# Leaky values kept in PSUM in the first block, and the last quadrant's ScalarE passes moved into the next slot

## The chip, the cores and the metric

The kernel runs on one NeuronCore of a Trainium2 chip. Its engines are TensorE (PE in the profile, its weight loads PEld), VectorE (DVE), ScalarE (ACT), GpSimd (POOL) and SyncE (SP, which issues most DMAs here). Each engine works through its own instructions in the order in which the program issues them, and waits on semaphores for the others. The metric is the device time of one execution in microseconds; before the change it is 1990.66 us, the median of three runs (1990.62 to 1990.68).

## The reference

A gated scan over time feeds a two-layer MLP with a leaky activation. In short:

```python
sig = 1.0 / (1.0 + np.exp(-f_logit))          # (4, 6080, 256)
f = lower_bound + (1.0 - lower_bound) * sig
h = f[:, t] * h + (1.0 - f[:, t]) * x[:, t]   # for t in range(6080); y[:, t] = h
x = y.reshape(24320, 256)
h = x @ w_in                                  # (256, 2048)
out = np.maximum(0.01 * h, h) @ w_out         # (2048, 256)
```

All of it is float32. The kernel reaches that precision on TensorE by splitting each operand into a high part (rounded to fp32r by a write of that type) and a low part (the value less its high part), and by summing three products: low weight by high value, high by high, high by low.

## The kernel before, in words

**Tiling.** The 24320 tokens are cut into 24 blocks of 1024 (the last has 768); a block's two halves of 512 are the columns of the matmuls. The 2048 hidden features are cut into 8 groups of 256. A *slot* is one group of one block; its hidden values are four *quadrants* of 128 features by 512 tokens, written (h, t) with h the feature half and t the token half. There are 192 slots, in order of block and group (the list `seq`, line 364).

**A quadrant's way.** Its sum h ends in a PSUM bank or an SBUF tile. Two ScalarE passes follow: `leaky_high` (L352) writes the leaky value rounded to fp32r, gh, to SBUF; `leaky` (L357) writes the leaky value in full float32. VectorE's `low` (L362) subtracts the two and gives gl. Six matmuls (`second`, L290) then take gh and gl to the output banks o. Three of a slot's four second products run in the next slot (`old`), one (0, 0) at the end of its own.

**Blocks 1 to 23 (`slot`, L428)** use a scheme of Strassen's kind: seven products M1 to M7 of three matmuls each (L268) instead of eight, over three banks a, b and c. PE's order in a slot is M1 (a), M5 (c), M2 (b), M6 (a), six matmuls of old (1, 1), M7 (a), six of old (1, 0), M4 (a), six of old (0, 1), M3 (c), six of second (0, 0). Bank a accumulates through M1, M6, M7 and M4; between them ScalarE copies the state to SBUF (c11 after M1, L438; c12 after M6, L445; c22 after M7, L450), so that M6 waits for c11's copy, M7 for c12's, M4 for c22's. VectorE adds the banks b and c to these (L442, L451, L469). The last quadrant (0, 1) is complete at L469, after M3; its passes stand at lines 473 and 474 and its low part at 476, at the end of the slot.

**The first block (`plain_slot`, L400, and `first_slots`, L530)** has no prepared sums of weights yet and takes eight plain products in each slot. In it the weights arrive: they are loaded raw, ScalarE prepares them in two passes (`scale_w`, L104 and L106), VectorE masks and joins them (`decode_w`, L112 and L113), POOL adds the two parts (L118), ScalarE rounds the high part (`split_w`, L127) and VectorE takes the low part (L129). For group g this is done for w_in of the next group and for w_out of its own. Also the weight sums for the later blocks are formed (`combine_w`, L134 to L138, and `split_c`, L144 and L145), one group in each slot from slot 6 of block 0 to slot 6 of block 1.

**Preparing the next block.** Transposes, gate, scan, differences and splits of block j + 1 are spread over the slots of block j by a table of hooks, keyed by slot and place. The places "C", "a0", "A", "W", "B", "a3", "D", "V" and "E" are calls in the slot's code. "a0" holds one ScalarE pass of 1024 columns in each of slots 2 and 3 (Tanh, L214) and 6 and 7 (rounding, L235). Block 0 uses the copy `late` of the table, with two places changed.

**The order** is written out by hand: inside `tc.manual_schedule()` every engine runs its instructions in the order of the code. Semaphores follow from which tile or bank is read and written. Tiles come from pools: a new tile of a tag takes the buffer that was given back first, and waits for its last reader. The tag "c" has four SBUF buffers, and in the program before c11 always lies where the previous slot's c11 lay, c12 where its c22 lay, c22 where its c21 lay. Bank a is a pair of PSUM buffers, b and c are one each; the output banks are four more.

Of the kernel before, what the change touches and what calls it, by code (L numbers as in the profile page):

```python
# [8 lines left out]
F32 = mybir.dt.float32  # L9
# [15 lines left out]
def tile_gated_scan_then_leaky_mlp(  # L25
# [13 lines left out]
    P = 128  # L39
# [54 lines left out]

    def scale_w(kind, g, hs=slice(0, 2)):
        if (kind, g) not in part_t:
            a = dw_p.tile([P, 2, 256], F32, tag="a", name="a", bufs=2)
            r = dw_p.tile([P, 2, 256], U32, tag="r", name="r")
            w = dw_p.tile([P, 4, P], F32, tag="w", name="w", bufs=2)
            part_t[kind, g] = a, r, w  # L100
        a, r, _ = part_t[kind, g]

        hi, lo = raw_t[kind, g][:, hs, :, 1], raw_t[kind, g][:, hs, :, 0]
        act(out=a[:, hs], in_=hi.bitcast(F32), func=ACTF.Abs, scale=2.0 ** -112)  # L104

        act(out=r[:, hs], in_=lo, func=ACTF.Copy, scale=2.0 ** -29)  # L106
# [22 lines left out]
            vtt(out=wl, in0=w, in1=wh.bitcast(F32), op=ALU.subtract)  # L129

    def combine_w(g):
        w = dw_p.tile([P, 4, P], F32, tag="a", name="a", bufs=2)
        c = dw_p.tile([P, 4, P], F32, tag="w", name="c", bufs=2)
        vtt(out=w, in0=wi_h[:, g, 0:4].bitcast(F32), in1=wi_l[:, g, 0:4].bitcast(F32), op=ALU.add)  # L134
        vtt(out=c[:, 0], in0=w[:, 2], in1=w[:, 3], op=ALU.add)
        vtt(out=c[:, 2], in0=w[:, 0], in1=w[:, 2], op=ALU.subtract)
        vtt(out=c[:, 1], in0=c[:, 0], in1=w[:, 0], op=ALU.subtract)
        vtt(out=c[:, 3], in0=w[:, 1], in1=c[:, 1], op=ALU.subtract)  # L138
        part_t["c", g] = c
# [114 lines left out]
    }  # L254
    late = dict(hooks)
    late[1, "E"] = late.pop((1, "A"))
    late[2, "A"], late[2, "E"] = hooks[2, "A"][:1], hooks[2, "A"][1:]

    hooks_own = {(0, "C"): [("l", (5, 7))]}

# [102 lines left out]

    seq = [(j, g) for j in range(NB) for g in range(NG)]

    def new_c():
        return c_p.tile([P, HM], F32, tag="c", name="c")

# [13 lines left out]
                    plain_halves(bank, j, g, h, t, k, order, rnd)  # L382

    def plain_leaky(j, g, h, t, bank):
        c = new_c()
        leaky_high((j, g, h, t), bank)
        leaky((j, g, h, t), c, bank)
        return c

    def plain_bank(h, t):  # L390
        pool, tag = (ps_b, "bc"[h == 0]) if t else (ps_a, "a")
# [8 lines left out]
    def plain_slot(s, hook):  # L400
        j, g = seq[s]
        hook("C")
        p11 = plain_quad(j, g, 0, 0)
        if s == 2:
            second(j, 1, 0, 0)
        c11 = plain_leaky(j, g, 0, 0, p11)
        hook("a0")
        hook("A")
        hook("W")
        old(s, 1, 1)  # L410
        low((j, g, 0, 0), c11)
        c22 = plain_leaky(j, g, 1, 1, plain_quad(j, g, 1, 1))
        hook("B")
        old(s, 1, 0)
        low((j, g, 1, 1), c22)
        c21 = plain_leaky(j, g, 1, 0, plain_quad(j, g, 1, 0))
        hook("a3")
        hook("D")
        old(s, 0, 1)
        low((j, g, 1, 0), c21)  # L420
        b = plain_quad(j, g, 0, 1)
        hook("V")
        c12 = plain_leaky(j, g, 0, 1, b)
        second(j, g, 0, 0)
        low((j, g, 0, 1), c12)
        hook("E")

    def slot(s, hook):  # L428
        j, g = seq[s]
        n = sizes[j] // 2  # L430
        done = g == 0 and j > 0
        a = ps_a.tile([P, HM], F32, tag="a", name="pa")
        b = ps_b.tile([P, HM], F32, tag="b", name="pb")
        c = ps_b.tile([P, HM], F32, tag="c", name="pc")
        product(a, j, g, M1, True)
        hook("C")
        c11 = new_c()
        act(out=c11[:, :n], in_=a[:, :n], func=ACTF.Copy)  # L438
        product(c, j, g, M5, True)
        product(b, j, g, M2, True)  # L440
        hook("a0")
        vtt(out=c11[:, :n], in0=b[:, :n], in1=c11[:, :n], op=ALU.add)  # L442
        product(a, j, g, M6, False)
        c12 = new_c()
        act(out=c12[:, :n], in_=a[:, :n], func=ACTF.Copy)  # L445
        hook("A")
        old(s, 1, 1)
        product(a, j, g, M7, False)
        c22 = new_c()
        act(out=c22[:, :n], in_=a[:, :n], func=ACTF.Copy)  # L450
        vtt(out=c22[:, :n], in0=c[:, :n], in1=c22[:, :n], op=ALU.add)  # L451
        leaky_high((j, g, 0, 0), c11)
        leaky((j, g, 0, 0), c11, c11)
        old(s, 1, 0)
        if done:
            evacuate(j - 1, 0)
        low((j, g, 0, 0), c11)
        hook("B")
        leaky_high((j, g, 1, 1), c22)
        leaky((j, g, 1, 1), c22, c22)  # L460
        low((j, g, 1, 1), c22)
        product(a, j, g, M4, False)
        c21 = new_c()
        leaky_high((j, g, 1, 0), a)
        leaky((j, g, 1, 0), c21, a)
        old(s, 0, 1)
        hook("a3")
        product(c, j, g, M3, False)
        vtt(out=c12[:, :n], in0=c[:, :n], in1=c12[:, :n], op=ALU.add)  # L469
        low((j, g, 1, 0), c21)  # L470
        if done:
            evacuate(j - 1, 1)
        leaky_high((j, g, 0, 1), c12)
        leaky((j, g, 0, 1), c12, c12)
        second(j, g, 0, 0)
        low((j, g, 0, 1), c12)
        hook("E")


# [50 lines left out]
    def first_slots(hook):  # L530

        j, g = 0, 0
        h0, h1 = slice(0, 1), slice(1, 2)
        keep_busy(5)
        turn_first(0, 0)
        keep_busy(2)
        turn_first(1, 0)
        keep_busy(4)
        scale_w("i", 0, h0)
        decode_w("i", 0, h0)  # L540
        gate_first(0, 0)
        u_first(0, 0)
        split_w("i", 0, "hl", h0)
        scale_w("i", 0, h1)
        scan_first(0, 0)
        decode_w("i", 0, h1)
        gate_first(1, 0)
        u_first(1, 0)
        high(0)
        lower(0)  # L550
        split_w("i", 0, "h", h1)
        p11, p21 = plain_bank(0, 0), plain_bank(1, 0)
        plain_halves(p11, j, g, 0, 0, 0, (1, 0, 2))
        turn_first(0, 1)
        scale_w("i", 1)
        scan_first(1, 0)
        split_w("i", 0, "l", h1)
        plain_halves(p21, j, g, 1, 0, 0, (1, 2, 0))
        turn_first(1, 1)
        high(1)  # L560
        lower(1)
        decode_w("i", 1)
        gate_first(0, 1)
        u_first(0, 1)
        gate_first(1, 1)
        u_first(1, 1)
        plain_halves(p11, j, g, 0, 0, 1)
        plain_halves(p21, j, g, 1, 0, 1)
        scan_first(0, 1)
        split_w("i", 1, "hl")  # L570
        scan_first(1, 1)

        q11, q21 = (ps_b.tile([P, HM], F32, tag=tag, name="p" + tag) for tag in "bc")
        keep_busy(3, q11)
        plain_rounds(((0, q11), (1, q21)), j, 1, 0, ((1, 2), (0,)))
        leaky_high((j, g, 0, 0), p11)
        high(3)
        c11 = new_c()
        leaky((j, g, 0, 0), c11, p11)
        high(2)  # L580
        lower(3)
        lower(2)
        p22, p12 = (ps_o.tile([P, HM], F32, tag=tag, name="p" + tag) for tag in ("o10", "o11"))
        plain_rounds(((1, p22), (0, p12)), j, g, 1, ((0, 1), (2,)))
        scale_w("o", 0)
        c21 = plain_leaky(j, g, 1, 0, p21)
        decode_w("o", 0)
        load_w("i", 2)
        load_w("o", 1)
        load(1, "l")  # L590
        load_w("o", 2)
        load(1, "x")
        low((j, g, 0, 0), c11)
        q22, q12 = (ps_a.tile([P, HM], F32, tag="a", name="pa") for _ in range(2))
        for h, q in ((1, q22), (0, q12)):
            for k in range(KC):
                plain_halves(q, j, 1, h, 1, k)
        c22 = plain_leaky(j, g, 1, 1, p22)
        low((j, g, 1, 0), c21)
        split_w("o", 0, "hl")  # L600
        scale_w("i", 2)
        decode_w("i", 2)
        load_w("i", 3)
        low((j, g, 1, 1), c22)
        c12 = plain_leaky(j, g, 0, 1, p12)
        low((j, g, 0, 1), c12)
        last_state(0, 0)
        last_state(0, 1)
        second(j, 0, 0, 0)
        hook("C")  # L610
        d11 = plain_leaky(j, 1, 0, 0, q11)
        hook("V")
        second(j, 0, 1, 0)
        d21 = plain_leaky(j, 1, 1, 0, q21)
        low((j, 1, 0, 0), d11)
        hook("W")
        second(j, 0, 1, 1)
        d22 = plain_leaky(j, 1, 1, 1, q22)
        low((j, 1, 1, 0), d21)
        second(j, 0, 0, 1)  # L620
        d12 = plain_leaky(j, 1, 0, 1, q12)
        low((j, 1, 1, 1), d22)
        low((j, 1, 0, 1), d12)
        hook("E")

    with tc.manual_schedule():
# [18 lines left out]
        for s in range(1, len(seq)):  # L645
            j, g = seq[s]

            def hook(at):
                if j == 0:

                    if at == "C":
                        scale_w("o", g)
                        decode_w("o", g)
                        if 1 < g < NG - 1:
# [68 lines left out]
```

## Time and profile before

| What | Value |
|---|---|
| Median of three runs | 1990.66 us |
| The profiled execution's own time | 1990.47 us |
| Its span, first to last instruction | 1988.7 us |
| PE busy | 1977.7 us, 99% of the span |
| PEld / DVE / ACT busy | 82% / 72% / 71% |
| POOL busy | 27.0 us, all in the first 100 us |
| Granted TensorE clock | 1.00 |

Times in the lines of the profile are microseconds from the first instruction, then the duration; "out<-in" names the tiles, and a bracket at the end gives the idle time of the engine before the instruction and what ended it. A matmul's duration includes the time in which it drains beside the next one, so the distance between starts tells what it costs: some 0.229 us for 512 columns. A slot of blocks 2 to 22 takes 10.30 us, 45 matmuls. In the list of groups a row gives the line, the engine, the operation, the tiles with shapes, the count, the busy time with the mean in ns, and the idle time before.

### The profile page before, as it was taken

Reading aid. Unit: us, or ns where it says so; the run is one execution under the profiler, and the core shown is the slowest. Engines: PE = TensorE matmul, PEld = TensorE weight load, DVE = VectorE, ACT = ScalarE, POOL = GpSimd, SP = SyncE. Lnnn points to the kernel's source line nnn. Section 1 sums busy time; section 2 is a strip of 40 time slices with the busy share of each in tenths; the row PEclk is TensorE's granted clock in tenths of the full one; section 3 lists DMA queues with packets and bytes.
Section 4 is the critical chain, followed back from the end, with each engine's and each line's share of the span. In section 5 each row is a group of like instructions: output and inputs, shape, how many; then the busy total and the mean of one; then the engine's idle time right before and its main releaser. Section 6 shows DMA issues by size and latency. Waiting matters only on the chain.

```text
span 1988.7 us, 23487 instructions
## 1 busy us (share of the span) xinstructions
PE 1977.7 (99%) x8820; PEld 1631.3 (82%) x8820; DVE 1422.2 (72%) x2001; ACT 1403.3 (71%) x2354; POOL 27.0 (1%) x25
## 2 busy tenths in 40 slices
PE   8999999999999999999999999999999999999999
PEld 7787888888888888888888888888888888888889
DVE  7987777776777767777677776777767767676664
ACT  7777677667776677766777767776677676776665
POOL 2300000000000000000000000000000000000000
PEclk9999999999999999999999999999999999999999
DMA  9650431504415144051450514505135042340110
GB/s 191 106 64 10 55 49 15 64 13 52 53 11 64 16 48 58 7 64 21 44 62 3 64 23 41 64 0 64 29 36 64 1 64 33 32 54 1 22 22 17
DMA packets 579010, 84.63 MB, mean 43 GB/s; under 512 B 567888, under 2 KB 576848, under 8 KB 578896
## 3 DMA queue, kind: packets, MB, share of 16 engines
q1 hardware_dynamic: 577552, 82.34, 32.7%
q8 instruction: 69, 1.13, 0.2%
q10 hardware_dynamic: 1344, 0.79, 0.1%
q14 instruction: 45, 0.37, 0.1%
HBM read 58.20 MB, written 24.90 MB: 42 GB/s over the span
## 4 chain that ended last, share of the span: by engine, by line
PE 97%; DVE 1%; ACT 0%; issue 0%; DMA 0%; POOL 0%; ACTq 0%; DVEq 0%; POOLq 0%
PE o L290 50%; PE pa L268 26%; PE pc L268 13%; PE pb L268 7%; PE o L309 2%; DVE gl L362 0%; DMA xld<-in_x_dram 0%; DVE xT L180 0%; DVE wi_l L129 0%; POOL w L118 0%; PE po L268 0%; DVE xT L211 0%; DVE lT L211 0%; DVE a L113 0%; PE po L507 0%
## 5 line engine op out<-in xcount | busy, mean ns | idle before, releaser
L290 PE MATMUL o<-gh,wo 128*128 128x512 f32 x2944 | 791.1, 391 | 0.0
L362 DVE TENSOR_TENSOR gl<-c,gh 128x512 fp32r<-128x512 f32 (+1 forms) x768 | 527.7, 691 | 280.9 <-ACT c L357 280.9
L290 PEld LDWEIGHTS o<-gh,wo 128*128 128x128 f32 x2944 | 552.8, 188 | 121.4
L352 ACT ACTIVATE gh<-c 128x512 fp32r<-128x512 f32 (+1 forms) x552 | 342.3, 620 | 168.6 <-DVE c L469 162.2
L290 PE MATMUL o<-gl,wo 128*128 128x512 f32 x1472 | 458.6, 393 | 0.0
L357 ACT ACTIVATE c<-c 128x512 f32<-128x512 f32 (+1 forms) x552 | 346.4, 627 | 17.5
L290 PEld LDWEIGHTS o<-gl,wo 128*128 128x128 f32 x1472 | 276.5, 188 | 59.8
L268 PE MATMUL pa<-yl,wi_h 128*128 128x512 f32 (+1 forms) x768 | 300.9, 392 | 0.1
L268 PE MATMUL pa<-yh,wi_l 128*128 128x512 f32 (+1 forms) x768 | 297.4, 387 | 3.0 <-ACT c L357 1.7
L268 PE MATMUL pa<-yh,wi_h 128*128 128x512 f32 (+1 forms) x768 | 299.5, 390 | 0.6 <-ACT yh L235 0.6
L450 ACT ACTIVATE c<-pa 128x512 f32<-128x512 f32 (+1 forms) x184 | 109.3, 594 | 181.4 <-PE pa L268 178.5
L445 ACT ACTIVATE c<-pa 128x512 f32<-128x512 f32 (+1 forms) x184 | 109.4, 594 | 181.2 <-PE pa L268 180.8
L451 DVE TENSOR_TENSOR c<-pc,c 128x512 f32<-128x512 f32 (+1 forms) x184 | 126.0, 685 | 99.0 <-ACT c L450 94.9
L442 DVE TENSOR_TENSOR c<-pb,c 128x512 f32<-128x512 f32 (+1 forms) x184 | 126.0, 685 | 92.0 <-PE pb L268 79.3
L469 DVE TENSOR_TENSOR c<-pc,c 128x512 f32<-128x512 f32 (+1 forms) x184 | 126.2, 686 | 74.0 <-PE pc L268 73.5
L268 PEld LDWEIGHTS pa<-yh,wi_l 128*128 128x128 f32 x768 | 144.2, 188 | 36.9 <-ACT c L357 2.1
L268 PEld LDWEIGHTS pa<-yh,wi_h 128*128 128x128 f32 x768 | 144.2, 188 | 32.7 <-ACT yh L235 0.7
L268 PEld LDWEIGHTS pa<-yl,wi_h 128*128 128x128 f32 x768 | 144.4, 188 | 28.0 <-DVE yl L238 0.5
L268 PE MATMUL pc<-yl,wi_h 128*128 128x512 f32 (+1 forms) x382 | 149.6, 392 | 0.0
L268 PE MATMUL pc<-yh,wi_h 128*128 128x512 f32 (+1 forms) x382 | 148.9, 390 | 0.0
L268 PE MATMUL pc<-yh,wi_l 128*128 128x512 f32 (+1 forms) x382 | 147.7, 387 | 0.0
L352 ACT ACTIVATE gh<-pa 128x512 fp32r<-128x512 f32 (+1 forms) x200 | 115.8, 579 | 5.2 <-PE pa L268 4.6
(96 smaller groups left out, 1758.9 us busy)
## 6 DMA issues: line engine op xcount, KB each, us to landing
out_dram<-osb SPq DMA_DIRECT2D x184, 128.0 KB, 3.2
lld<-in_f_logit_dram SPq DMA_DIRECT2D x91, 256.0 KB, 5.9
xld<-in_x_dram SPq DMA_DIRECT2D x91, 256.0 KB, 5.8
rawld<-in_moe_w_out_dram SPq DMA_DIRECT2D x6, 512.0 KB, 4.6
raw<-in_moe_w_in_dram SPq DMA_DIRECT2D x8, 256.0 KB, 4.5
rawld<-in_moe_w_in_dram SPq DMA_DIRECT2D x8, 256.0 KB, 3.0
raw<-in_moe_w_out_dram SPq DMA_DIRECT2D x2, 512.0 KB, 3.7
lld<-in_f_logit_dram SPq DMA_DIRECT2D x4, 192.0 KB, 4.5
```

The source lines that it names most:

```text
L268: nc.tensor.matmul(out=bank[:, :n], lhsT=a[:, g, w, :], rhs=b[:, i, :n], start=start and e == 0, stop=stop and e == len(order) - 1, skip_g ...
L290: nc.tensor.matmul(out=o[k][:, :n], lhsT=wo[:, g, h, w, k * P:(k + 1) * P], rhs=v[:, :n], start=first and s == 0, stop=last and s == 2, sk ...
L309: nc.tensor.matmul(out=o[:, u % 2 * D:(u % 2 + 1) * D], lhsT=v[:, u * P:(u + 1) * P], rhs=wo[:, g, h, w, :],  start=first and e == 0 and u ...
L352: act(out=gh[:, :n], in_=src[:, :n], func=ACTF.Prelu, alpha=0.01)
L357: act(out=dst[:, :n], in_=src[:, :n], func=ACTF.Prelu, alpha=0.01)
L362: vtt(out=gl[:, :n], in0=c[:, :n], in1=gh[:, :n].bitcast(F32), op=ALU.subtract)
L442: vtt(out=c11[:, :n], in0=b[:, :n], in1=c11[:, :n], op=ALU.add)
L445: act(out=c12[:, :n], in_=a[:, :n], func=ACTF.Copy)
L450: act(out=c22[:, :n], in_=a[:, :n], func=ACTF.Copy)
L451: vtt(out=c22[:, :n], in0=c[:, :n], in1=c22[:, :n], op=ALU.add)
L469: vtt(out=c12[:, :n], in0=c[:, :n], in1=c12[:, :n], op=ALU.add)
```

## The change

Four things change.

In the first block, `leaky` writes its full value back into the PSUM bank that it reads, and `low` reads it there; no tile of the tag "c" is used for it. The bank then stays in use until `low` has read it. In `plain_slot` the low part of quadrant (0, 0) is issued right behind its passes, ahead of the hooks "a0", "A" and "W".

The tiles a and r of `scale_w` take buffers of the tag "c" instead of tags of their own (r had one buffer, a two), and the tag "a", now used by `combine_w` alone, has one buffer.

In slot 1 of block 0 the calls of the hooks "C", "V" and "W" are written out: the split of w_in 2 now stands ahead of the decoding of w_out 1 and of the first pair of passes, where it stood behind these passes. In slot 2 of block 0 the two transposes of x move from place "E" to place "A".

In blocks 1 to 23 the passes and the low part of quadrant (0, 1) are put into a list `late_c` and issued in the next slot: the passes right behind c11's copy, the low part right behind L442. The last slot of all keeps the old place.

```diff
     def scale_w(kind, g, hs=slice(0, 2)):
         if (kind, g) not in part_t:
-            a = dw_p.tile([P, 2, 256], F32, tag="a", name="a", bufs=2)
-            r = dw_p.tile([P, 2, 256], U32, tag="r", name="r")
+            a = c_p.tile([P, 2, 256], F32, tag="c", name="a")
+            r = c_p.tile([P, 2, 256], U32, tag="c", name="r")
...
     def combine_w(g):
-        w = dw_p.tile([P, 4, P], F32, tag="a", name="a", bufs=2)
+        w = dw_p.tile([P, 4, P], F32, tag="a", name="a")
...
     late[1, "E"] = late.pop((1, "A"))
-    late[2, "A"], late[2, "E"] = hooks[2, "A"][:1], hooks[2, "A"][1:]
...
     def plain_leaky(j, g, h, t, bank):
-        c = new_c()
         leaky_high((j, g, h, t), bank)
-        leaky((j, g, h, t), c, bank)
-        return c
+        leaky((j, g, h, t), bank, bank)
+        return bank
...
-        c11 = plain_leaky(j, g, 0, 0, p11)
+        low((j, g, 0, 0), plain_leaky(j, g, 0, 0, p11))
         hook("a0")
         hook("A")
         hook("W")
         old(s, 1, 1)
-        low((j, g, 0, 0), c11)
...
         act(out=c11[:, :n], in_=a[:, :n], func=ACTF.Copy)
+        for key, src in late_c:
+            leaky_high(key, src)
+            leaky(key, src, src)
         product(c, j, g, M5, True)
         product(b, j, g, M2, True)
         hook("a0")
         vtt(out=c11[:, :n], in0=b[:, :n], in1=c11[:, :n], op=ALU.add)
+        for key, src in late_c:
+            low(key, src)
+        late_c.clear()
         product(a, j, g, M6, False)
         c12 = new_c()
         act(out=c12[:, :n], in_=a[:, :n], func=ACTF.Copy)
...
-        leaky_high((j, g, 0, 1), c12)
-        leaky((j, g, 0, 1), c12, c12)
-        second(j, g, 0, 0)
-        low((j, g, 0, 1), c12)
+        if s + 1 < len(seq):
+            second(j, g, 0, 0)
+            late_c.append(((j, g, 0, 1), c12))
+        else:
+            leaky_high((j, g, 0, 1), c12)
+            leaky((j, g, 0, 1), c12, c12)
+            second(j, g, 0, 0)
+            low((j, g, 0, 1), c12)
         hook("E")
...
-        c11 = new_c()
-        leaky((j, g, 0, 0), c11, p11)
+        leaky((j, g, 0, 0), p11, p11)
...
-        hook("C")
+        scale_w("o", 1)
+        split_w("i", 2, "hl")
+        decode_w("o", 1)
         d11 = plain_leaky(j, 1, 0, 0, q11)
-        hook("V")
         second(j, 0, 1, 0)
         d21 = plain_leaky(j, 1, 1, 0, q21)
         low((j, 1, 0, 0), d11)
-        hook("W")
+        split_w("o", 1, "hl")
```

More of the change, by code (lines that the diff above doesn't have):

```diff
@@ L364, in tile_gated_scan_then_leaky_mlp @@
     seq = [(j, g) for j in range(NB) for g in range(NG)]
+    late_c = []
     def new_c():
@@ L592, in first_slots @@
         load(1, "x")
-        low((j, g, 0, 0), c11)
+        low((j, g, 0, 0), p11)
         q22, q12 = (ps_a.tile([P, HM], F32, tag="a", name="pa") for _ in range(2))
@@ L649, in hook @@
                 if j == 0:
-                    if at == "C":
+                    if at == "C" and g > 1:
                         scale_w("o", g)
```

## The prediction

> **What bounds the kernel now.** I read the page first (the share of each engine), then who waited for whom on PE, then busy time by stretch, and last the timeline around each wait of PE.
>
> ```profile
> span 1988.7 us, 23487 instructions
> PE 1977.7 (99%) x8820; PEld 1631.3 (82%) x8820; DVE 1422.2 (72%) x2001; ACT 1403.3 (71%) x2354; POOL 27.0 (1%) x25
> ...
> PE pa L268 <- DVE wi_l L129: 1.2, 1, 1.2
> PEld pa L268 <- ACT c L438: 2.1, 5, 0.5
> PEld pc L268 <- DVE c L451: 0.9, 3, 0.4
> ...
> 186.80:1834.80 1648.00, 1648.00 (x7202) 1352.25 (x7201) 1171.08 (x1607) 1164.39 (x1921) 0.00 (x0) 1.00 0.33 39
> ```
>
> PE sets the time. In blocks 2 to 21 (the last row) it is busy all 1648.00 us, so nothing can be won there; what a change can win are the few waits in blocks 0 and 1. A wait costs more than the idle time shown, and this event of block 1 gives the rule:
>
> ```profile
> 124.60 0.58 ACT L438 ACTIVATE c<-pa 128x512 f32<-128x512 f32 x1
> ...
> 124.94 0.40 PE L268 MATMUL pb<-yl,wi_h 128*128 128x512 f32 x1
> ...
> 125.23 0.19 PEld L268 LDWEIGHTS pa<-yh,wi_l 128*128 128x128 f32 x1 [0.33 <-ACT c L438]
> ...
> 125.57 0.39 PE L268 MATMUL pa<-yh,wi_h 128*128 128x512 f32 x1
> ```
>
> ScalarE's copy ends at 125.18 and the weight load that waits for it starts 0.05 later. A matmul follows the one before at 0.229 (0.46 for the two at 1035.01, below); here two took 125.57 - 124.94 = 0.63 where 0.46 is due: 0.17 lost. So a weight load that starts L after the last matmul's start delays PE by L - 0.12 (0.29 - 0.12). By the starts of the matmuls the five waits on L438 cost 1.29 and two on L451 0.38 (the groups' idle, 2.1 and 0.9, less 0.16 for each event), together **1.67 us in block 1**.
>
> **The part in later blocks, which decides.** A full slot of block 2 and later, on ScalarE (ACT) and PE (this is slot 2 of a block):
>
> ```profile
> 1030.90 0.63 ACT L352 ACTIVATE gh<-c 128x512 fp32r<-128x512 f32 x1 [0.91 <-DVE c L469]
> 1031.57 0.63 ACT L357 ACTIVATE c<-c 128x512 f32<-128x512 f32 x1
> 1031.81 0.39 PE L268 MATMUL pa<-yl,wi_h 128*128 128x512 f32 x1
> 1032.24 0.60 ACT L438 ACTIVATE c<-pa 128x512 f32<-128x512 f32 x1
> 1032.73 1.05 ACT L214 ACTIVATE lT<-lT 128x1024 f32<-128x1024 f32 x1
> 1034.30 0.60 ACT L445 ACTIVATE c<-pa 128x512 f32<-128x512 f32 x1 [0.51 <-PE pa L268]
> 1035.01 0.62 PE L290 MATMUL o<-gl,wo 128*128 128x512 f32 x2
> 1035.24 0.19 PEld L268 LDWEIGHTS pa<-yh,wi_l 128*128 128x128 f32 x1
> 1035.47 0.39 PE L268 MATMUL pa<-yh,wi_l 128*128 128x512 f32 x1
> 1037.51 0.63 ACT L357 ACTIVATE c<-c 128x512 f32<-128x512 f32 x1
> 1038.05 0.62 ACT L352 ACTIVATE gh<-c 128x512 fp32r<-128x512 f32 x1
> ...
> 94.07 2.01 ACT L235 ACTIVATE yh<-lT 128x1024 fp32r<-128x1024 f32 x2
> 95.96 0.72 ACT L144 ACTIVATE wi_h<-c 128x128 fp32r<-128x128 f32 x2
> ```
>
> Before, the last quadrant's two passes (1030.90, 1031.57) lie ahead of the copy c11 (L438), in time in which ScalarE has nothing else: the copy starts at 1032.24, 0.04 after M1's last matmul ends (1031.81 + 0.39), so PE sets it. Taking the passes from in front of it wins nothing here.
>
> After, they stand between that copy and the hook "a0", and the hook's 1024-wide pass and then the copy c12 (L445) queue behind them. From start to start: copy to next 0.49 (1032.24 to 1032.73); first pass to second 0.66 (it waits for the end, 1030.90 to 1031.57); second pass to the next 0.54 (1037.51 to 1038.05); a 1024-wide pass 0.94 (1.89 for two, 94.07 to 95.96). So c12's copy starts at 1032.24 + 0.49 + 0.66 + 0.54 + 0.94 = 1034.87 instead of 1034.30, and ends 0.60 later, at 1035.47.
>
> Product M7 writes the bank that this copy reads, and its weight load stands at 1035.24, with the last matmul before it started at 1035.01 + 0.23 = 1035.24. Now the load starts at 1035.47 + 0.05 = 1035.52: L = 0.28, and PE loses 0.28 - 0.12 = **0.16 us**. Without a pass in the hook the copy could start 0.94 sooner, at 1033.93, before M6 ends, and nothing is lost.
>
> The hook "a0" holds such a pass in slots 2, 3 (Tanh, L214) and 6, 7 (L235) of each block that prepares a full next block. Rows of blocks 2 to 21:
>
> ```profile
> L235 ACT ACTIVATE yh<-lT 128x1024 fp32r<-128x1024 f32 x40 | 42.1, 1052 | 0.0
> L214 ACT ACTIVATE lT<-lT 128x1024 f32<-128x1024 f32 x40 | 42.1, 1052 | 0.0
> L235 ACT ACTIVATE yh<-xT 128x1024 fp32r<-128x1024 f32 x20 | 21.0, 1052 | 0.0
> ```
>
> In "a0" are all 40 Tanh, the 20 of yh<-xT and half of the 40 of yh<-lT (the other half is in "A", behind c12's copy): 80 slots, 80 x 0.16 = **+12.8 us**. In block 22 the next block is three quarters as long, its pass at least 0.2 shorter, and the loss is gone.
>
> Nothing makes up for it: PE has no other wait there, and every later step of a slot moves with PE. On VectorE the late low part (L362) goes behind L442 and pushes the hook "A" back by 0.6; in slot 5 L451 then comes some 0.6 later, but M3, which needs it, has about 1 us of room. The quadrant's gh and gl are read only by the next slot's second-last group of matmuls, over 3 us after the late pass.
>
> **Block 1.** Its waits on L438 go, since the copy no longer stands behind passes that wait for a late VectorE; VectorE starts each slot's sums 0.6 or more sooner, which ends the two on L451: -1.67. The same M7 loss comes in slots 2, 3, 6, 7: +0.64. In slots 2 and 3 there is more behind c12's copy:
>
> ```profile
> 126.73 1.23 ACT L217 ACTIVATE lT<-lT,cd,cc 128x1024 f32<-128x1024 f32 x1
> 127.87 0.71 ACT L144 ACTIVATE wi_h<-c 128x128 fp32r<-128x128 f32 x2
> ```
>
> From c12's copy start to c22's copy it is then 0.49 + 1.14 + 0.61 = 2.24, 0.59 past M7's end, and M4 waits for it: +0.18 each. Block 1: -1.67 + 0.64 + 0.36 = **-0.67**.
>
> **Block 0.** The rows:
>
> ```profile
> 15.60 1.28 POOL L118 TENSOR_TENSOR w<-a,r 128x512 uint32<-128x512 uint32 x1 [4.41 <-ACT lT L511]
> 16.34 0.69 DVE L517 SCALAR_TENSOR_TENSOR xT<-lT,po 128x512 f32<-128x512 f32 x1 [0.31 <-ACT lT L512]
> ...
> 26.59 2.39 DVE L362 TENSOR_TENSOR gl<-c,gh 128x512 fp32r<-128x512 f32 x2
> 26.85 1.59 POOL L118 TENSOR_TENSOR w<-a,r 128x512 uint32<-128x512 uint32 x1 [2.62 <-DVE a L113]
> 29.18 3.35 SPq L156 DMA_DIRECT2D xld<-in_x_dram  x2
> 30.32 1.30 POOL L118 TENSOR_TENSOR w<-a,r 128x512 uint32<-128x512 uint32 x1 [1.88 <-DVE a L113]
> 30.98 0.63 PE L290 MATMUL o<-gl,wo 128*128 128x512 f32 x2
> 33.31 0.50 PE L268 MATMUL pa<-yh,wi_l 128*128 128x512 f32 x1 [1.70 <-ACT c L357]
> 45.99 0.19 PEld L268 LDWEIGHTS pa<-yh,wi_l 128*128 128x128 f32 x1 [0.48 <-DVE wi_l L129]
> 102.51 0.69 DVE L362 TENSOR_TENSOR gl<-c,gh 128x512 fp32r<-128x512 f32 x1 [0.56 <-ACT c L357]
> 103.19 0.39 PE L268 MATMUL pc<-yh,wi_l 128*128 128x512 f32 x1
> ...
> xld<-in_x_dram SPq DMA_DIRECT2D x91, 256.0 KB, 5.8
> ```
>
> A low part with both inputs in SBUF that meets POOL's sum takes 1.7 to 1.8 (the pair at 26.59 takes 2.39) and stretches POOL to 1.59; a VectorE instruction with one input in PSUM runs in 0.69 beside POOL's 1.28. With its values in PSUM the low part gets that second price, and POOL 1.30. Against it: the second pass, in place, now waits for the first (0.03 behind its end, not 0.10 ahead: +0.14 each), and a bank is free only after the low part, not after the pass.
>
> By rows the first wait, at 33.31, grows: POOL's sum for w_in 2 ends at 28.15, its split on ScalarE 28.18 to 28.81, on VectorE 28.87 to 29.55; now VectorE's two steps for w_out 1 come behind that, to 30.62, POOL 30.78 to 32.08 (before to 31.62), the split of w_out 1 on ScalarE 32.11, passes of quadrant 22 32.64 and 33.25 to 33.84, and on VectorE, behind the w_out split and one low part, the low part that frees the bank 34.00 to 34.69. Weight load 34.74 instead of 33.31: loss 34.74 - 31.21 - 0.12 = 3.41 instead of 1.98. The waits at 45.99 (0.33) and 58.44 (1.46) go: the w_in splits end at about 46.4 and 57.6, PE wants them at 47.2 and 58.2. Adding 0.03 at the bank of p11: -0.33. At 103.19 product M5 takes the bank of the last quadrant, whose low part ends at 103.20; PE and the passes come 0.35 sooner and 0.13 later, so M5 now waits about +0.29. The earlier r pass (its tile no longer waits for POOL) and the two transposes are in these times. The transposes come some 7 us sooner, at about 39.5, ahead of the w_out 2 split on VectorE, which holds back POOL's w_in 3 to 43.6 to 44.9 (its split is the 46.4 above); no DMA moves with them, and the x load that they need is issued by 32.53 and lands some 5.8 after its issue, by 38.4. Without that room PE would wait there for what is missing. Block 0: **-0.04**. What has no row is the pass from PSUM to PSUM: rows have 0.59 out of PSUM and 0.63 out of SBUF; I take 0.59, bounds 0.55 and 0.63, a few hundredths on each link, with other slips -0.7 to +1.0 for the block.
>
> **Sum:** 12.8 - 0.67 - 0.04 = +12.1. The profiled execution took 1990.47 (1.77 more than its span), the median of the runs shown is 1990.66; so 2002.6 to 2002.8: **2002.7 us**, 0.6% slower.
>
> **Rivals.**
> - *Hidden after all* (not slower). Place: M7's weight load, in 80 slots. If ScalarE's line from c11's to c12's copy is 0.16 shorter than counted (each of its five steps 0.03), the load is in time: 1990.66 - 1.67 - 0.04 = 1988.95. For it: 0.16 is little beside a line of 3.2. Against: its pitches repeat within 0.02 over hundreds of slots. 10%.
> - *A buffer wait*. c12's new tile would take the buffer that the late low part still reads: from L442's start 2.32 after M1's, low part 2.93 to 3.61, copy 3.64 to 4.24 where 3.96 is in time: 0.28 in 175 full slots, +49 in place of 13.4: 2038. Against: in the program before, the new c12 takes the buffer of the previous slot's c22, which is long free. 4%.
> - *A slow clock* after the long pause at 31 to 34.7: should PE run at half pitch for as long as it paused, some 13 matmuls cost 0.23 more each, +3.0: 2005.7. Against: the 1.70 pause before left the next matmuls at 0.39, with the granted clock 1.00. 5%. The Trainium skill, "TensorE: Matmul & The Clock Gate", section "Why this matters for your kernels", asks for no pause over about 3 us, or the clock falls to half; the trace before has no pause that long.
> - *All waits gone, nothing added*: 3.77 in block 0 and 1.67 in block 1 off: 1985.2, the floor. 2%.
>
> **How the numbers follow.** The forecast has 79%. Its own range: 0.12 to 0.20 in 80 slots is 9.6 to 16.0, with blocks 0 and 1 within -0.7 to +1.5: 1998.8 to 2007.4. 0.2% is 4 us, about what can be told from no change. Slower by more: the forecast, the buffer wait, the slow clock, 88%; within: the hidden case, 10%; faster by more: 2%. The range 1998 to 2008 leaves out the hidden case, the buffer wait and the floor, 16%.
>
> **What would show it.** Right: in slots 2, 3, 6, 7 of each block a wait of pa's weight load on ACT L445, 80 or more times, and the other slots at 10.30; no waits on L438; one longer wait at 31 us, now on VectorE's L362; L362 near 0.69 in block 0. Wrong: no wait on L445, or one in all slots (then the buffer).

## The result, and the profile after

The changed kernel takes **2003.67 us** (median of 6, 2002.03 to 2005.97) against 1990.68 for the kernel before beside it (median of 6): a ratio of 1.0066, 95% interval 1.0055 to 1.0076. It is 0.66% slower; predicted were 2002.7 and slower. The profiled execution took 2003.66, its span is 2001.9. Among the runs below, one execution took far longer than its nine fellows (2025.11, with the late passes in half the slots); no trace shows why, and the ratio given there leaves it out.

In the profile after, the helpers' lines are one lower than before: L267 is the products, L289 the second products, L351 and L356 the two passes, L361 the low part. In a slot c11's copy is L438 as before, c12's is L451 (was L445), c22's L456 (was L450). First come two lines of the page, and then the waits of PE's weight loads that the change made or altered (idle time of the load in us, number, longest):

```profile
span 2001.9 us, 23578 instructions
PE 1990.7 (99%) x8820; PEld 1626.0 (81%) x8820; DVE 1384.4 (69%) x2001; ACT 1375.5 (69%) x2354; POOL 22.2 (1%) x25
```

```profile
PEld pa L267 <- ACT c L451: 25.0, 84, 0.3
PEld pa L267 <- DVE gl L361: 3.6, 2, 3.4
...
PEld pa L267 <- ACT c L456: 0.6, 2, 0.3
PEld pc L267 <- DVE gl L361: 0.3, 1, 0.3
```

The five waits on c11's copy and the three on VectorE's sum (two of which had cost PE time) are gone, and 84 waits on c12's copy are new: 80 in blocks 2 to 21 and 4 in block 1. PE still counts as busy for 99%, because the wait of a weight load hides in the drain of the matmul before it; its busy time grew from 1977.7 to 1990.7 with the same 8820 matmuls.

How much they cost, by the first copy c11 of blocks 1, 2 and 22, in the timeline of before and then of after:

```profile
103.44 0.60 ACT L438 ACTIVATE c<-pa 128x512 f32<-128x512 f32 x1 [0.96 <-ACT c L357]
...
187.64 0.60 ACT L438 ACTIVATE c<-pa 128x512 f32<-128x512 f32 x1
...
1835.64 0.60 ACT L438 ACTIVATE c<-pa 128x512 f32<-128x512 f32 x1
```

```profile
104.61 0.60 ACT L438 ACTIVATE c<-pa 128x512 f32<-128x512 f32 x1 [0.92 <-PE pa L267]
...
188.14 0.60 ACT L438 ACTIVATE c<-pa 128x512 f32<-128x512 f32 x1 [2.24 <-PE pa L267]
...
1848.80 0.60 ACT L438 ACTIVATE c<-pa 128x512 f32<-128x512 f32 x1 [2.24 <-PE pa L267]
```

From block 2 to 22 it was 1648.00 and is 1660.66: **+12.66, or 0.158 for each of the 80 slots**. Block 1 is 0.67 shorter (83.53 for 84.20). Up to block 1 the kernel has lost 1.17. The rest, blocks 22 and 23, is the same: the end is 13.2 later.

One of the 80 slots, on ScalarE and at product M7:

```profile
1039.07 0.60 ACT L438 ACTIVATE c<-pa 128x512 f32<-128x512 f32 x1 [2.24 <-PE pa L267]
1039.57 0.62 ACT L351 ACTIVATE gh<-c 128x512 fp32r<-128x512 f32 x1
1040.22 0.63 ACT L356 ACTIVATE c<-c 128x512 f32<-128x512 f32 x1
1040.76 1.05 ACT L214 ACTIVATE lT<-lT 128x1024 f32<-128x1024 f32 x1
1041.71 0.57 ACT L451 ACTIVATE c<-pa 128x512 f32<-128x512 f32 x1
1041.85 0.62 PE L289 MATMUL o<-gl,wo 128*128 128x512 f32 x2
1042.18 1.23 ACT L217 ACTIVATE lT<-lT,cd,cc 128x1024 f32<-128x1024 f32 x1
1042.34 0.19 PEld L267 LDWEIGHTS pa<-yh,wi_l 128*128 128x128 f32 x1 [0.29 <-ACT c L451]
```

The steps 0.50, 0.65, 0.54 and 0.95 are the four that the prediction added up (0.49, 0.66, 0.54, 0.94): from c11's copy to c12's 2.64, where 2.63 was predicted. The copy ends at 1042.28 and the load starts 0.06 later. The last matmul ahead of it starts at 1041.85 + 0.23 = 1042.08, so L is 0.26, and the prediction's rule (L - 0.12) gives 0.14 for this slot; the four such slots of a block lose 0.15 to 0.17 by their lengths.

In block 0 the pause of PE is there, and behind it something that had been given 5%. PE after the pause, and the granted clock in stretches of 1 us (stretch, length, busy time of PE, PEld, DVE, ACT and POOL, each with its number of instructions, then PEclk, the share of the DMA engines and GB/s):

```profile
31.09 0.63 PE L289 MATMUL o<-gl,wo 128*128 128x512 f32 x2
34.70 0.50 PE L267 MATMUL pa<-yh,wi_l 128*128 128x512 f32 x1 [2.99 <-DVE gl L361]
...
35.97 0.57 PE L267 MATMUL pa<-yl,wi_h 128*128 128x512 f32 x1
36.33 1.91 PE L289 MATMUL o<-gh,wo 128*128 128x512 f32 x4
38.04 1.05 PE L289 MATMUL o<-gl,wo 128*128 128x512 f32 x2
38.89 1.35 PE L289 MATMUL o<-gh,wo 128*128 128x512 f32 x4
40.08 0.63 PE L289 MATMUL o<-gl,wo 128*128 128x512 f32 x2
```

```profile
35.00:36.00 1.00, 1.00 (x6) 0.78 (x5) 1.00 (x2) 0.83 (x2) 0.00 (x0) 1.00 1.60 131
36.00:37.00 1.00, 1.00 (x4) 0.81 (x3) 1.00 (x2) 0.00 (x0) 0.00 (x0) 0.51 1.48 137
37.00:38.00 1.00, 1.00 (x3) 0.75 (x3) 1.00 (x2) 0.00 (x0) 0.00 (x0) 0.50 1.10 209
38.00:39.00 1.00, 1.00 (x4) 0.77 (x3) 0.71 (x2) 0.72 (x2) 0.09 (x1) 0.50 1.10 355
39.00:40.00 1.00, 1.00 (x5) 0.82 (x4) 0.60 (x1) 1.00 (x2) 1.00 (x1) 0.78 1.02 375
```

Four matmuls from 36.33 to 38.04 are 1.71, 0.427 each, where 0.229 is due. The clock is granted at half from 36.0 to about 39.4, and by the matmuls' starts (from 35.97 to 40.08 eleven matmuls, 4.11 for 2.52) this costs 1.59.

### The profile page after: what moved, and what is told of

The parts are those of the page before. It is cut to its first block, busy times and chain, and to the rows that moved or that the text cites. A ratio compares the mean times of both kernels' runs of the same rounds, so it can differ in the third digit from the quotient of the medians.

```text
span 2001.9 us, 23578 instructions
## 1 busy us (share of the span) xinstructions
PE 1990.7 (99%) x8820; PEld 1626.0 (81%) x8820; DVE 1384.4 (69%) x2001; ACT 1375.5 (69%) x2354; POOL 22.2 (1%) x25
## 4 chain that ended last, share of the span: by engine, by line
PE 98%; ACT 0%; DMA 0%; DVE 0%; POOL 0%; issue 0%; ACTq 0%; POOLq 0%
PE o L289 50%; PE pa L267 26%; PE pc L267 13%; PE pb L267 7%; PE o L308 2%; DMA xld<-in_x_dram 0%; POOL w L118 0%; PE po L267 0%; ACT lT L522 0%; DMA out_dram<-osb 0%; ACT lT L521 0%; DVE a L113 0%; ACT wi_h L127 0%; ACT wo L127 0%; DVE xT L180 0%
## 5 line engine op out<-in xcount | busy, mean ns | idle before, releaser
L289 PE MATMUL o<-gh,wo 128*128 128x512 f32 x2944 | 794.8, 392 | 0.0
L289 PEld LDWEIGHTS o<-gh,wo 128*128 128x128 f32 x2944 | 553.7, 188 | 121.4
L361 DVE TENSOR_TENSOR gl<-c,gh 128x512 fp32r<-128x512 f32 (+1 forms) x736 | 497.6, 679 | 134.1 <-ACT c L356 132.4
L289 PE MATMUL o<-gl,wo 128*128 128x512 f32 x1472 | 457.4, 392 | 0.0
L438 ACT ACTIVATE c<-pa 128x512 f32<-128x512 f32 (+1 forms) x184 | 109.3, 594 | 394.7 <-PE pa L267 394.7
L356 ACT ACTIVATE c<-c 128x512 f32<-128x512 f32 (+1 forms) x552 | 346.5, 628 | 17.5
L445 DVE TENSOR_TENSOR c<-pb,c 128x512 f32<-128x512 f32 (+1 forms) x184 | 126.1, 685 | 326.4 <-PE pb L267 323.0
L351 ACT ACTIVATE gh<-c 128x512 fp32r<-128x512 f32 (+1 forms) x552 | 340.8, 617 | 7.0 <-DVE c L457 6.4
L289 PEld LDWEIGHTS o<-gl,wo 128*128 128x128 f32 x1472 | 276.7, 188 | 61.6
L267 PE MATMUL pa<-yh,wi_l 128*128 128x512 f32 (+1 forms) x768 | 308.5, 402 | 3.0 <-DVE gl L361 3.0
L267 PE MATMUL pa<-yl,wi_h 128*128 128x512 f32 (+1 forms) x768 | 300.4, 391 | 0.2 <-DVE yl L238 0.2
L267 PE MATMUL pa<-yh,wi_h 128*128 128x512 f32 (+1 forms) x768 | 298.7, 389 | 0.6 <-ACT yh L235 0.6
L456 ACT ACTIVATE c<-pa 128x512 f32<-128x512 f32 (+1 forms) x184 | 109.3, 594 | 149.9 <-PE pa L267 147.6
L267 PEld LDWEIGHTS pa<-yh,wi_l 128*128 128x128 f32 x768 | 144.1, 188 | 55.2 <-ACT c L451 25.0
L267 PEld LDWEIGHTS pa<-yl,wi_h 128*128 128x128 f32 x768 | 144.3, 188 | 31.1 <-DVE yl L238 0.6
L267 PEld LDWEIGHTS pa<-yh,wi_h 128*128 128x128 f32 x768 | 144.3, 188 | 28.4 <-ACT yh L235 0.8
L267 PE MATMUL pc<-yl,wi_h 128*128 128x512 f32 (+1 forms) x382 | 149.2, 391 | 0.0
L267 PE MATMUL pc<-yh,wi_l 128*128 128x512 f32 (+1 forms) x382 | 148.6, 389 | 0.0
L267 PE MATMUL pc<-yh,wi_h 128*128 128x512 f32 (+1 forms) x382 | 148.2, 388 | 0.0
L451 ACT ACTIVATE c<-pa 128x512 f32<-128x512 f32 (+1 forms) x184 | 107.3, 583 | 26.6 <-PE pa L267 25.8
```

The costliest lines, as they stand in the source:

```text
L267: nc.tensor.matmul(out=bank[:, :n], lhsT=a[:, g, w, :], rhs=b[:, i, :n], start=start and e == 0, stop=stop and e == len(order) - 1, skip_g ...
L289: nc.tensor.matmul(out=o[k][:, :n], lhsT=wo[:, g, h, w, k * P:(k + 1) * P], rhs=v[:, :n], start=first and s == 0, stop=last and s == 2, sk ...
L351: act(out=gh[:, :n], in_=src[:, :n], func=ACTF.Prelu, alpha=0.01)
L356: act(out=dst[:, :n], in_=src[:, :n], func=ACTF.Prelu, alpha=0.01)
L361: vtt(out=gl[:, :n], in0=c[:, :n], in1=gh[:, :n].bitcast(F32), op=ALU.subtract)
```

## The experiments

My theory: M7's 0.158 comes from one queue, ScalarE's, in which c12's copy stands behind the two late passes and the hook's 1024-wide pass, and it is the whole loss of the later blocks. The rivals: that it comes from the late passes as such, or a buffer, whatever stands in the hook; that the PSUM part of block 0 holds a loss of its own; and for the 4 us between the executions of the changed kernel, that the slow clock after the pause is behind them. The diffs are against the changed kernel unless the text says otherwise. Beside the first four the kernel before took 1990.83, beside the rest 1990.89 or 1990.90.

**Block 0 alone** (the last quadrant keeps its old place):

```diff
-        if s + 1 < len(seq):
-            second(j, g, 0, 0)
-            late_c.append(((j, g, 0, 1), c12))
+        if False:
+            pass
         else:
```

> The last quadrant keeps its old place in blocks 1 to 23; the changes of the first block stay. Theory (the loss is the copy c12 queueing behind two passes and a 1024-wide one): no weight load waits for L451 in any slot, blocks 2 to 21 are as before, 10.30 us a slot; what is left is block 0's +1.2 (with the slow clock after the pause, -0.4 without), +0.2 at M5 of block 1, and block 1's old waits: 1990.7 to 1992.1 us. Rival (the loss in later blocks comes with the first block's changes, for instance through the four shared buffers of tag c): about 2003 as with the whole change.

1992.03 (median of 10, 1990.2 to 1994.27), ratio 1.0007 (0.9997 to 1.0016).

```profile
PEld pa L267 <- DVE gl L361: 3.6, 2, 3.4
PEld pa L267 <- ACT c L438: 1.7, 4, 0.5
...
PEld pc L267 <- DVE c L457: 0.9, 3, 0.4
```

No wait on L451 is left and blocks 2 to 21 take 82.40 each again, as before. Block 1 takes 84.20 as before: four of its five waits on c11's copy are still there, and the one of M5 has come in. What block 0 costs differs from execution to execution: two of the ten kept a mean clock of 1.000 and took 1990.20 and 1990.42, which is 0.4 to 0.6 less than the kernel before beside them, where the prediction had -0.04; the profiled one, with 0.998, took 1993.1, and in it the half clock lasts from 34.1 to 40.9 us. Four of the ten lie inside the expected range, four above it (to 1994.27) and two below.

**The late passes alone** (the kernel before, with the list `late_c`):

> Only the last quadrant's move; the first block as before. Theory: 80 waits of 0.16 in blocks 2 to 21, +12.7, block 1 some -0.8, no long pause at 31 us and so no slow clock in any execution: 2002.6 us, and executions that lie as close together as the kernel's before. Rival (the spread of 2002.0 to 2006.0 seen with the whole change comes from the late passes): a spread of some us here too.

2002.36 (4 executions, 2002.30 to 2002.52), ratio 1.0058 (1.0043 to 1.0073); c12's copy is L453 here:

```profile
PEld pa L268 <- ACT c L453: 25.0, 84, 0.3
```

The same 84 waits of the same 25.0 us, and a block of 83.02 for 82.40. So the loss belongs to this part alone: +11.5 here, 20 x 0.62 = 12.4 less the 0.9 that block 1 gains (83.28 for 84.20). The spread is 0.22, against 3.94 of the changed kernel: so what scatters comes with the changes of block 0.

**Late only into slots without a pass in "a0":**

```diff
-        if s + 1 < len(seq):
+        if s + 1 < len(seq) and (g + 1) % NG in (0, 1, 4, 5):
```

> The last quadrant is moved only where the next slot is 0, 1, 4 or 5 of its block, those without a 1024-wide pass in the hook a0; elsewhere it keeps its old place. Theory: no loss at M7 anywhere, 12.7 us of the 13.2 in blocks 2 to 21 gone, block 1 keeps its waits in slots 2, 3 and 6 (0.18, 0.17, 0.31) and loses those of 4 and 5: 1990.9 us, or 1.6 less in executions without the slow clock. Rival (moving the passes costs PE something in every slot, with or without the hook's pass, for instance through the late low part): half of the loss stays, about 1997.

1990.45 (median of 10, 1989.16 to 2025.11), ratio 0.9998 (0.9988 to 1.0007). The profiled execution took 1989.2. Its waits of PE's weight loads, those on DMAs and on the first block's inputs left out:

```profile
PEld pa L267 <- DVE gl L361: 3.6, 2, 3.4
...
PEld pc L267 <- DVE gl L361: 0.3, 1, 0.3
PEld pa L267 <- ACT c L438: 0.3, 1, 0.3
PEld pc L267 <- DVE c L457: 0.2, 1, 0.2
```

No weight load waits for c12's copy, though half of all slots still take the late passes. So neither the late passes by themselves nor a buffer is the cause; it takes the hook's wide pass in the same stretch. In block 1 one wait on c11's copy is left, where three were expected to stay.

**The passes apart**, the second and the low part further back in the slot:

```diff
             leaky_high(key, src)
-            leaky(key, src, src)
...
-        for key, src in late_c:
-            low(key, src)
-        late_c.clear()
         product(a, j, g, M6, False)
         c12 = new_c()
         act(out=c12[:, :n], in_=a[:, :n], func=ACTF.Copy)
+        for key, src in late_c:
+            leaky(key, src, src)
...
         vtt(out=c22[:, :n], in0=c[:, :n], in1=c22[:, :n], op=ALU.add)
+        for key, src in late_c:
+            low(key, src)
+        late_c.clear()
```

> The last quadrant's first pass stays behind c11's copy, its second pass goes behind c12's copy and its low part behind L451. Theory by the same row times: c12's copy could start at 0.49 + 0.53 + 0.94 = 1.96 after c11's copy, earlier than M6's end allows (2.06), so no wait at M7 in any slot of blocks 2 to 21; c22's copy comes 0.1 late in slots 2 and 3, which M4 does not see; in block 1 slots 2 and 3 M4 waits 0.3 each: 1991 us. Rival (any pass between c11's and c12's copy costs): some +6 left.

1991.32 (median of 10, 1989.47 to 1992.42), ratio 1.0002 (0.9993 to 1.0012). All slots take the late passes, no wait on c12's copy is left, and every block from 2 to 21 takes 82.40. One pass (some 0.6) less ahead of the copy is more than the 0.16 that was missing. In block 1 M4 waits twice, at 0.34 each by the starts, as expected. The change wins nothing over the kernel before, since there was nothing to win in these blocks.

**One pass more ahead of the copy** (the first late pass is issued twice with the same result):

> The whole change, with the last quadrant's first pass issued twice behind c11's copy (the same values again). Theory (the sum of ScalarE's passes ahead of c12's copy decides): the copy comes 0.53 to 0.66 later, in 80 slots of blocks 2 to 21 and 4 of block 1 the wait grows from 0.16 to 0.69 to 0.82, and in slots without a pass in the hook a0 the copy ends 0.1 before it is needed, so nothing is lost there: 2003.7 + 84 x 0.53 to 0.66 = 2048 to 2059 us. Rival (the wait has a fixed size, as of a buffer or of VectorE): 2003.7. A wait in every slot would give 100 us or more.

One execution, 2062.7. In a slot of block 13 (L442 is the doubled pass, L453 c12's copy):

```profile
1068.44 0.60 ACT L438 ACTIVATE c<-pa 128x512 f32<-128x512 f32 x1 [1.97 <-PE pa L267]
...
1069.59 0.63 ACT L442 ACTIVATE gh<-c 128x512 fp32r<-128x512 f32 x1
...
1071.74 0.57 ACT L453 ACTIVATE c<-pa 128x512 f32<-128x512 f32 x1
```

```profile
PEld pa L267 <- ACT c L453: 84.0, 89, 1.0
```

From copy to copy it is 3.30 for 2.64, and a block 85.66 for 83.03: 0.66 more in each of four slots. What is put into that queue is paid in full, and in the four slots with a wide pass: 88 of the 89 waits stand there, the last one (0.3 of idle load) in the last block. The time is 4 above the expected range: 84 x 0.66 = 55.4 on 2003.67 makes 2059.1, and block 22, whose hook passes are a quarter shorter, which keeps it clear in the changed kernel, now pays too: 84.64 for 82.27, +2.4. The rest, 1.2, is less than the 3.94 by which the executions of the changed kernel differ, and one execution can't tell more.

**The pause filled** (12 matmuls of 512 columns into a free bank, whose result nothing reads, behind the last second product of the stretch):

> The whole change, with twelve more matmuls of 512 columns (2.75 us) on bank b in the pause of TensorE at 31 us, whose result nothing reads; they wait for the low part that frees bank b at 31.2 and are done before the bank of the next slot is free at 34.7. Theory of the clock (a pause of 3 us lowers the granted clock to half for some us): no slow clock, matmuls at 0.23 throughout, the time of the executions without it, 2002.0 us, and executions within 0.3 us of each other. Rival (the slow stretch comes from something else at this point, as the DMAs in flight): it stays, about 2003.7 with a spread of some us.

2001.69 (4 executions, 2001.56 to 2001.91), ratio 1.0054 (1.0039 to 1.0069).

```profile
31.66 2.91 PE L636 MATMUL pad<-yh,wi_h 128*128 128x512 f32 x12
34.83 0.50 PE L267 MATMUL pa<-yh,wi_l 128*128 128x512 f32 x1 [0.26 <-DVE gl L361]
...
36.33 0.85 PE L289 MATMUL o<-gh,wo 128*128 128x512 f32 x3
```

PE is kept from its useful work just as long (from 31.66 to 34.83; in the changed kernel from 31.55 to 34.70), but it isn't idle, and the clock stays at 1.00 in every stretch from 30 to 42 us. The 84 waits are unchanged (24.9 us). Against the changed kernel it is 2.0 less and the spread falls from 3.94 to 0.35. The long wait itself stays, so the difference is the half clock, and the idle pause is its cause.

**A shorter pause** (slot 1 of block 0 in the order of before, where the decoding of w_out 1 stands ahead of the split of w_in 2):

```diff
         scale_w("o", 1)
-        split_w("i", 2, "hl")
         decode_w("o", 1)
         d11 = plain_leaky(j, 1, 0, 0, q11)
+        split_w("i", 2, "hl")
```

> The whole change, but in slot 1 of block 0 the split of w_in 2 stands behind the first pair of passes and the decoding of w_out 1 ahead of them, as before. Theory (the first wait grew because VectorE's steps for w_out 1 queue behind the split of w_in 2, and because the bank is held until the low part): the bank is free at about 33.6 instead of 34.65, the wait costs 2.2 instead of 3.3, the pause is too short for the slow clock: 2001 us with a small spread. Rival (the bank held by the low part alone makes the wait): no change in the wait.

2001.53 (2002.21, 2002.31, 2000.66, 2000.86), ratio 1.0053 (1.0039 to 1.0067).

```profile
33.90 0.52 PE L267 MATMUL pa<-yh,wi_l 128*128 128x512 f32 x1 [1.91 <-DVE gl L361]
34.24 0.61 PE L267 MATMUL pa<-yh,wi_h 128*128 128x512 f32 x1
34.64 0.63 PE L267 MATMUL pa<-yl,wi_h 128*128 128x512 f32 x1
```

The pause is 1.1 shorter (1.91 of idle PE for 2.99), and the wait costs 2.18 by the starts, as expected: the order of VectorE's steps is part of it. I had taken such a pause for too short to slow the clock, and it isn't: in the profiled execution the matmuls follow each other at 0.40 to 0.43 from 34.24 on, and the four times fall into two pairs 1.5 apart. The upper pair shows a mean clock of 0.999, the lower pair 1.000.

**The waits taken out.** Late passes only into slots 4, 5 and 6 of block 1, where M6 had waited longest for c11's copy (0.31 to 0.32 by the starts, twice the 0.16 that slot 6 then pays at M7); slot 1 of block 0 as in the last run, with quadrant (1, 1) second and its full value in SBUF, so that its bank is free after the pass; and the full value of block 0's last quadrant in SBUF too:

```diff
-        if s + 1 < len(seq):
+        if j == 1 and g in (3, 4, 5):
...
-        d21 = plain_leaky(j, 1, 1, 0, q21)
+        d22 = plain_leaky(j, 1, 1, 1, q22, new_c())
         low((j, 1, 0, 0), d11)
+        low((j, 1, 1, 1), d22)
         split_w("o", 1, "hl")
```

> What the theory says would beat both. The last quadrant moves only into slots 4, 5 and 6 of block 1. The first block keeps its values in PSUM, but in slot 1 quadrant (1, 1) comes second, its full value goes to SBUF (the bank is then free after the pass, 30.8, before TensorE wants it at 31.4), the decoding of w_out 1 stands ahead of the split of w_in 2; and the last quadrant of slot 7 goes to SBUF too (M5 of block 1 then finds its bank free). Theory: block 0 loses its 3.77 us of waits, M5 none, block 1 keeps 0.18, 0.17 and 0.16 of 1.67: 1990.8 - 3.8 - 1.2 = 1985.8 us, ratio 0.9975. Rival (the waits taken away come back at the next slots' weight splits, since ScalarE and VectorE have as much to do): 1988 to 1990.

**1987.16** (median of 11, 1987.00 to 1987.63), ratio 0.9982 (0.9973 to 0.9990): faster than both kernels. PE runs through from 30 to 42 us with the clock at 1.00; the wait of before at 33.31 is gone. 1.4 of the expected gain is missing, and the trace shows where:

```profile
45.24 0.51 PE L267 MATMUL pa<-yh,wi_l 128*128 128x512 f32 x1 [0.96 <-DVE wi_l L129]
```

PE now comes to slot 3 some 1.7 us sooner than in the kernel before, and w_in 3 isn't split by then; 1.24 comes back by the starts. M6 keeps 0.18 in each of slots 2 and 3 of block 1.

**The transposes back at "E"** (the kernel of the last run, with the line `late[2, "A"], late[2, "E"] = ...` of before):

> The kernel of the run before (late passes only into slots 4, 5 and 6 of block 1, slot 1 of block 0 reordered), with the two transposes of x in slot 2 of block 0 at place "E" again instead of "A". In that run's trace VectorE does both transposes from 38.32 to 40.68, ahead of the low part of w_out 2 (40.61) and of the two steps for w_in 3 (41.18, 41.64); POOL's sum follows at 42.50, the low part wi_l of w_in 3 at 44.49, and PE waits for it at 45.24, losing 1.24. If it is these 2.3 us of VectorE that are late, wi_l comes at 42.2 to 43, the wait goes and nothing takes its place: 1987.16 - 1.24 = 1985.9, range 1985.5 to 1986.5. If ScalarE or POOL hold wi_l back on their own account, or if what the transposes feed becomes late in slot 3 or 4, a wait of 0.3 to 1.3 stays in 44 to 60 us: 1986.3 to 1987.3.

1988.31 (median of 11, 1988.00 to 1989.07), ratio 0.9987 (0.9978 to 0.9996): 1.15 slower than without. The expectation fell. In the profiled execution the split of w_in 3 is no sooner: VectorE's first step for it now waits for ScalarE's scaling pass (L104) in place of the transposes, and that pass waits for the load of w_in 3 from DRAM. The later wait, before at 58.44 with 1.46, is there again. The scaling pass, VectorE's first step, and then PE:

```profile
40.80 0.66 ACT L104 ACTIVATE a<-raw 128x512 f32<-128x512 f32 x1 [0.82 <-DMA raw<-in_moe_w_in_dram]
...
41.49 0.43 DVE L112 TENSOR_SCALAR raw<-raw 128x512 uint32<-128x512 uint32 x1 [0.78 <-ACT a L104]
```

```profile
45.55 0.50 PE L268 MATMUL pa<-yh,wi_l 128*128 128x512 f32 x1 [1.23 <-DVE wi_l L129]
...
58.21 0.51 PE L268 MATMUL pa<-yh,wi_l 128*128 128x512 f32 x1 [1.39 <-DVE wi_l L129]
```

The profiled execution is the slowest of the eleven, and in it the SyncE queue issued that load 1.7 us later than in the run before (34.44 for 32.77, in both before any of the moved transposes runs), where ScalarE did not wait for it. So the first wait, 1.50 here, is not shown to be as long in the other ten, and whether the transposes alone hold w_in 3 back stays open. For the second wait the runs are clear: among the changes of block 0 it is the place of the transposes that takes out the wait at 58.44; without it the others, as they stand in this kernel, leave it there.

## Why the prediction was right, and where it wasn't

**The later blocks** were right as worked out. 80 waits of 0.16 in slots 2, 3, 6 and 7 were predicted, +12.8; measured are 80 of 0.158, +12.66. The steps of ScalarE agree within 0.01 each and 0.01 in their sum. That the sum of ScalarE's passes ahead of the copy decides, and that it takes the wide one to make it too long, is shown from three sides: without the late passes in these four slots no wait is left, with one pass less ahead of the copy none is left, with one more each wait grows by the 0.66 of that pass. The *hidden* rival needed 0.16 of slack that isn't there; the *buffer* rival would have shown waits in all slots.

**Block 1** was predicted from its first copy c11 to its end at -1.67 + 0.64 + 0.36, and M5's +0.29, which the prediction booked under block 0, falls into the same stretch: -0.38. Measured is -0.67. The waits that were to go are gone; M7 waits four times, M4 twice (0.6 us of idle loads in all) and M5 once (0.3), as named. M5 costs 0.18 by the starts, not 0.29, and M4 0.15, not 0.18; that is 0.17 of the 0.29 by which the block came out better, and the other 0.12 was not traced.

**Block 0.** Up to the first c11 the prediction has -0.33 (-0.04 less M5's 0.29). Counted from the last pair of matmuls ahead of the pause it was 103.44 - 30.98 = 72.46 and is 104.61 - 31.09 = 73.52: +1.06, of which 1.59 is the slow clock. Without that it is -0.53. In the run with late passes only into half the slots the clock stayed at 1.00 in the profiled execution, and the same stretch shows it directly:

```profile
31.55 0.62 PE L289 MATMUL o<-gl,wo 128*128 128x512 f32 x2
35.14 0.51 PE L267 MATMUL pa<-yh,wi_l 128*128 128x512 f32 x1 [2.97 <-DVE gl L361]
...
103.45 0.60 ACT L438 ACTIVATE c<-pa 128x512 f32<-128x512 f32 x1 [0.92 <-PE pa L267]
```

103.45 - 31.55 = 71.90, that is -0.56. The pieces: the first wait costs 3.27 by the starts, predicted 3.41; the two later ones are gone, as predicted; a low part beside POOL's sum takes 0.68 and POOL 1.30, the price that was taken. One step failed. The second pass, in place in PSUM, was to wait for the end of the first, +0.14 each. It doesn't:

```profile
28.73 0.58 ACT L351 ACTIVATE gh<-pb 128x512 fp32r<-128x512 f32 x1
29.20 0.59 ACT L356 ACTIVATE pb<-pb 128x512 f32<-128x512 f32 x1
```

It starts 0.47 after the first, 0.11 before that one ends, although it overwrites the bank that the first one reads; in SBUF, at 1039.57 and 1040.22 above, the same pair is 0.65 apart. The rule came from SBUF rows and was carried over to PSUM, for which there was no row. It cost the sum next to nothing, because VectorE's queue sets the low part that frees the bank: it starts at 33.97, predicted 34.00. Of the 0.14 by which the wait was overrated, 0.11 are that PE's last pair starts at 31.09 in this execution, and not at 30.98. The price of 0.59 for a pass from PSUM to PSUM is right. One sentence of the prediction is too general: that a wait costs more than the idle time shown holds for the idle time of PE (here 3.27 for 2.99), while a weight load's idle time is more than the cost (0.33 for 0.17 in the prediction's own event).

**The slow clock** was priced at +3.0 and given 5%, with the argument that the pause of before left no trace. It came in five of the six executions of the changed kernel (mean clock 0.999 or 0.998, 2003.45 to 2005.97 us); the one with 1.000 took 2002.03. A mean clock of 0.999 alone would not prove it, since three executions of the kernel before show it with ordinary times, but here clock and time agree. Predicted without it was 2002.7. That the median came out 1.0 from the prediction is therefore two errors that partly cancel: the rest came out 0.7 better than the sum, and the clock took about 1.6 back. As a chance, 5% was far too little; as a price, 3.0 was too much for most executions, though 2005.97 comes near it. The Trainium skill, "TensorE: Matmul & The Clock Gate", section "Why this matters for your kernels", had spoken for it: no pause over about 3 us. Here 2.99 of idle halved the clock in most executions and not in all, and 1.91, which that rule would let pass, halved it in two of four; the measurement decides.

## What to carry to other kernels

A copy that PE waits for is as late as everything that its own engine issues ahead of it: before work is moved "to where the engine is free", add up the starts from the last thing that is on time to the next copy that must be, slot by slot, with the widest hook in it. Where the bounding engine has no wait in a stretch, nothing can be won there, so such a move belongs only in the slots that do wait: three slots of block 1 here. An idle pause on PE can cost more than its length, and here filling it with matmuls that nothing reads got that back.

## What was not expected of the hardware

The clock halves behind a pause, with a delay that differs and for a time that differs: in the changed kernel from 1.3 us after PE starts again, for 3.4 us; with block 0 alone from 34.1, before PE starts again at 34.98, to 40.9; with the shorter pause from the second matmul on. An idle of 2.97 did it in the profiled execution of the run with block 0 alone and did not in that of the run with half the slots; 1.91 did it in half of the executions, and the 1.70 of before in none that shows in its times (1990.53 to 1991.16 beside the later runs).

The traces suggest what decides. The record of the granted clock begins, with the full clock, at its own moment in each execution, at 8.6 to 11.7 us in the eleven traces, and each later change of the clock lies a whole number of steps of 3.41 us behind that moment. In the changed kernel it begins at 8.72, the clock falls eight steps later at 36.02, and it is full again one step later at 39.44. Cut into these steps, the pauses look like this:

| Run | Step (us) | PE idle within the step | Clock behind it |
|---|---|---|---|
| One pass more | 32.08 to 35.49 | 3.00 | half |
| Passes apart | 32.14 to 35.55 | 2.86 | half |
| Changed kernel | 32.61 to 36.02 | 2.09 | half |
| Block 0 alone | 30.67 to 34.08 | 2.07 | half |
| Shorter pause | 30.83 to 34.24 | 1.91 | half |
| Half the slots, first step | 30.44 to 33.85 | 1.69 | full |
| Half the slots, second step | 33.85 to 37.27 | 1.29 | full |
| Late passes alone | 30.82 to 34.23 | 1.68 | full |
| Kernel before | 29.71 to 33.12 | 1.52 | full |

The clock fell behind the steps with 1.91 us or more of idle, and behind none with 1.69 or less. The same pause of 2.97 was cut into 2.07 and 0.90 with block 0 alone, and into 1.69 and 1.29 in the run with half the slots; there no step had enough idle. With block 0 alone, where 0.90 of idle stands in the next step, the half clock lasted two steps, elsewhere one. Since the steps begin at another moment in each execution, this would also make executions of one kernel differ. It is read from one trace of each kernel and tested by no run of its own.

A pass of ScalarE that overwrites a PSUM bank started 0.11 before the end of the pass ahead of it, which reads that bank (29.20 for 29.31), while the same pair on an SBUF tile was 0.03 apart (1040.22 for 1040.19).
